# Block 0's inverse taken straight from the four products, pairs formed later, in a two-layer convolution and GeGLU kernel

## The chip, the cores and the metric

The kernel runs on one core of one Trainium2 chip. The metric is the device time of one execution in microseconds (us), lower is better. Each core has TensorE (PE: matrix multiplies from SBUF into PSUM), VectorE (DVE), ScalarE (ACT), GpSimd (POOL) and a queue of its own for transfers (SP). SBUF is the on-chip memory, PSUM the memory that matmuls accumulate into; the program holds three PSUM tiles of one kind (`ps`, `pr`) and one of another (`cps`).

## The reference

```python
x = A_q
x = x + A(layernorm(x)); x = x + B(layernorm(x))
x = x + A(layernorm(x)); x = x + B(layernorm(x))

A(q):  k_shift = sum over 4 taps of k (delayed by t) * shift_k[:, t]
       kv = k_shift * v
       y = causal convolution of kv with ssm_k, by FFT of length 2S, in bf16
       return q * (y + kv * ssm_D)
B(x):  return (gelu(x @ w_gate) * (x @ w_up)) @ w_down
```

S is 2048 and D is 576; the hidden width F is 4608. `y` doesn't depend on x, so the kernel computes it once for both layers. The operands are bf16.

## The kernel before

**Tiling.** The sequence is cut into four chunks of 512 rows, and each chunk into four tiles of 128 rows. The convolution works by chunk: a block's `kv` and a block's filter are taken to a frequency domain of four tables of 128 frequencies (`kt` 0 to 3, each with a real and an imaginary part, `part` or `s` 0 and 1), multiplied there, and taken back by `inverse` (L392), one row tile `mt` at a time. Forward and backward transforms are matmuls with constant tables `W`; some of them also stand in `W` with the sign turned.

**Units.** The MLP runs in 8 units (two layers, four chunks). In a unit, `gu` (L1583 for the first unit's first third, L1663 for the others) multiplies the normed, transposed rows `xnT` by gate and up weights, ScalarE takes the gelu, VectorE the product `hT`, and `dn` (L1697) multiplies by the down weights. Weights stream in over SP's queue (`load_wgu`, `load_wd`). From the first `gu` on, the convolution of the later chunks is filled into these units by a planner (`Pace`, `fill`) with cost figures of its own; the change gives the planner no new figure.

**The opening.** Ahead of the first `gu` the program runs `begin` (L817), in an order written out by hand; each engine works through its instructions in that order. It computes block 0 of the convolution (which needs only chunk 0 of k, v and the filter), turns the filter's block 1, and brings rows 0 and 2 of chunk 0 through gate, norm and transpose, since the first half of the first unit needs only those (rows 1 and 3 follow in `first_half`, L1520). Its steps:

- `even` and `odd` (L973, L980): the filter's spectrum for two tables, from even and from odd rows, into one PSUM tile; ScalarE copies out the even sum `eo` and then the total `h`, and `apart` (L985) gets the other table by `differ` (L230, VectorE): twice the even sum less the total. `kfwd` (L990) is the same for `kv`, copied out by ScalarE as `kc`.
- `kacc(kt)` (L1000) forms the complex product of `kc` and `h` for one table: two tiles `A[(part, kt)]`, each a product (L358 or L360) and a sum (L361) on VectorE.
- `straight` (L1014) accumulates rows 0 and 2 of the inverse from the four `A` tables, as they come, in PSUM tiles `Y[0]` and `Y[2]`.
- `pair0(kt, sg)` (L1007) forms on GpSimd, for both parts, the sum (`sg` 0) or the difference (`sg` 1) of `A[(part, kt)]` and `A[(part, kt + 2)]`. Rows 1 and 3 of the inverse are taken from the two differences by `terms` (L385): 8 matmuls a row. The four differences and four sums (`yb`) also serve later: block 1's inverse needs the pairs of the block before it, which `shifted` (L378) updates in place, one of them by an adding transfer.
- `gate` (L1471; two multiply-adds on VectorE, L1478 and L1481), `mean`, `sq` (ScalarE, L1204), `std` (ScalarE, L1498), `norm` (VectorE, L1422, and a small copy, L1424), `turn` (nine transposes on TensorE, L1443) and `copy` (L1450) bring a row to `xnT`. `keep_y` (L406, ScalarE) copies a finished row of the inverse out of PSUM. `busy` (L871) and `idle` (L1431) are matmuls and transposes whose results are not used.
- `turn_h(1)` and `copy_h` transpose the filter's block 1 into `hT1`. `put` writes spectra to DRAM over GpSimd's queue.

**After it.** `first_half` runs six `half_gu` units of 36 matmuls. Each takes one of the three PSUM tiles, as do the two transposed rows between the third, fourth and fifth of them; of the first four units VectorE's product (L1589) is the last to read the tile.

Of the kernel before, what the change touches and what calls it, by code (L numbers as in the profile page):

```python
# [85 lines left out]
class Conv:  # L86
# [283 lines left out]
    def both(self, kt, part, first, second):  # L370

        b = {}
        for sg, op in ((0, ALU.add), (1, ALU.subtract)):
            b[sg] = self.ybp.tile([P, self.D], BF16, tag="yb", name="yb")
            self.nc.vector.tensor_tensor(out=self.halves(b[sg][:]), in0=first, in1=second, op=op)
        return b

    def shifted(self, now, prev, part, transfer=False):  # L378
        if transfer and part == 1:
# [437 lines left out]
    def begin(self, head, tables):  # L817
# [4 lines left out]
        with ExitStack() as es:  # L822
# [8 lines left out]
            ones = tmp.tile([1, P], BF16, name="ones")  # L831
            warm = tmp.tile([P, 1], F32, name="warm")
            self.Wx = tmp.tile([P, 2, P], BF16, name="Wx")
            hn = [tmp.tile([P, nd + 1, BS], BF16, name=f"hn{b}") for b in range(2)]
            hT0 = tmp.tile([P, RT, D], BF16, name="hT0")
            kT = head.scratch([P, nt, RT, P + 2], "kT")
# [99 lines left out]
            def turn_h(b):  # L936

                hv = hn[b][:].rearrange("p b (q i) -> p b i q", i=RT)
                pt = [new_t() for g in range(2)]
# [10 lines left out]
            copy_h(hT0, turn_h(0), (0, 1))  # L950
# [29 lines left out]
            def odd(kt, s):  # L980
                ps, eo = E[kt, s]
                self.fwd_sum(ps, hT0, kt, s, 1)
                nc.scalar.copy(out=self.halves(h0[kt][:, s, :]), in_=ps[:, :, 0:HW])

            def apart(kt):  # L985
                for s in range(2):
                    ps, eo = E[kt, s]
                    self.differ(h0[kt + 2][:, s, :], eo, ps)

            def kfwd(kt, s, ps):  # L990
                if s == 0:
                    kc[kt] = self.kcp.tile([P, 2, D], BF16, tag="kc", name="kc")
                self.fwd_full(v, kt, s, kc[kt], ps=ps)

            def put(kt, *what):
                for w in what:
                    self.spill((self.Kd if w is kc else self.Hd)[0][kt], w[kt])
                self.flush(0.0)
# [5 lines left out]
                    A[(part, kt)] = t  # L1004
            self.yb, self.yb_of = {}, 0

            def pair0(kt, sg):  # L1007
                for part in range(2):
                    b = self.ybp.tile([P, D], BF16, tag="yb", name="yb")
                    nc.gpsimd.tensor_tensor(out=b[:], in0=A[(part, kt)][:], in1=A[(part, kt + 2)][:],  # L1010
                                            op=ALU.subtract if sg else ALU.add)
                    self.yb[(part, kt, sg)] = b

            def straight(mt, kts, first=False, last=False):  # L1014

                self.inverse(0, mt, [(self.inv_w(mt, s, mt == 2 and kt % 2 == 1), A[(s, kt)]) for kt in kts for s in range(2)],
                             Y[mt], first, last)

            even(0, 0)
            even(0, 1)  # L1020
            kfwd(0, 0, small())
            odd(0, 0)
            odd(0, 1)
            kfwd(0, 1, new())
            head.row_sum(0)
            head.row_sum(2)
            apart(0)
            head.row_sum(1)
            head.act_sq(0)
            kacc(0)  # L1030
# [11 lines left out]
            odd(1, 0)  # L1042
            odd(1, 1)
            kfwd(1, 1, new())
            pair0(0, 1)
            apart(1)
            kacc(1)
            put(1, h0, kc)
# [2 lines left out]
            head.act_sq(2)  # L1051
            kfwd(3, 1, new())
            self.load_v(1, nc.gpsimd)
            self.hT1 = head.scratch([P, RT, D], "hT1")
            copy_h(self.hT1, turn_h(1), (1, 0))
            Y = {0: new()}
            head.reserve(0)
            Y[2] = new()
            straight(0, (0, 2), True)
            straight(2, (0, 2), True)  # L1060
            straight(0, (1,))
            kacc(3)
# [30 lines left out]
            nc.scalar.activation(out=warm[:], in_=head.zero, func=ACT.Gelu_apprx_tanh)  # L1093
            pair0(0, 0)
            pair0(1, 0)
            head.gate(1, None, 0)
            self.startup = False


@with_exitstack  # L1100
def ssm_geglu_kernel(ctx, tc, A_q, A_k, A_v, A_shift_k, A_ssm_k, A_ssm_D, B_x, B_w_gate, B_w_up,
# [308 lines left out]
    with tc.manual_schedule():  # L1410
# [377 lines left out]
```

## Time and profile before

| | before |
|---|---|
| time, median of 3 runs | 921.23 us (920.99 to 921.79) |
| the profiled execution's own time | 921.34 us |
| its span, first to last instruction | 919.5 us |
| TensorE, VectorE, ScalarE, GpSimd busy | 906.3, 584.0, 331.0, 165.8 us |
| first `gu` matmul | at 45.56 us of the span |
| chain that ended last | TensorE 95%, VectorE 4% |
| mean granted TensorE clock | 0.994 |

Rows of the profile name an engine, a line of the kernel, an operation and its tiles: `out<-in`, then partitions x elements and type, then how many instructions the row holds. A row of the timeline begins with its start and its length in us; square brackets hold the idle time of the engine before it, with the instruction that ended it. The chain of waits is followed back from the last instruction, at each step to what released it. Time on engines that the chain does not pass costs nothing by itself. "Granted clock" is the share of full speed that TensorE was allowed.

### The profile page before, as it was taken

To read this page: it belongs to the slowest core of one execution; us is meant where nothing else is said; L and a number is where in the kernel's file an instruction comes from. 1 tells how busy PE (TensorE), PEld (TensorE's weight loads), DVE (VectorE), ACT (ScalarE), POOL (GpSimd) and SP (SyncE) were. 2 spreads that over 40 slices of the span, in tenths; PEclk is the share of its full clock that TensorE was granted. 3 is DMA by queue.
4 is the path that set the end of the run, shared out by engine and by line. 5 is a ranking of instruction groups with operands and counts; after the bars stand their busy time and mean duration, and the time that the engine had idled before them with its cause. 6 is when DMAs were issued, how large, how long until landed. Compare 5 with 4: busy or idle time off the path is not lost.

```text
span 919.5 us, 19224 instructions
## 1 busy us (share of the span) xinstructions
PE 906.3 (99%) x8167; PEld 527.4 (57%) x8167; DVE 584.0 (64%) x973; ACT 331.0 (36%) x619; POOL 165.8 (18%) x341
## 2 busy tenths in 40 slices
PE   9699999999999999999999999999999999999998
PEld 6487456465564564655645646646546556556555
DVE  7988897679889886597898864453333335332332
ACT  7465724633215145363123133551221224421211
POOL 3711423311114022240103102220000003100000
PEclk9899999999999999999999999999999999999999
DMA  9759997929627707993933810890720721977620
GB/s 257 264 192 219 321 234 134 251 91 218 182 79 153 215 1 141 243 159 69 263 96 99 182 43 27 157 179 2 155 78 1 155 79 24 165 174 169 143 64 26
DMA packets 128954, 131.14 MB, mean 143 GB/s; under 512 B 43618, under 2 KB 120675, under 8 KB 128868
## 3 DMA queue, kind: packets, MB, share of 16 engines
q1 hardware_dynamic: 119232, 93.47, 48.3%
q0 software_dynamic: 9632, 36.43, 12.2%
q8 instruction: 64, 1.05, 0.5%
q14 instruction: 22, 0.18, 0.1%
q10 hardware_dynamic: 4, 0.01, 0.0%
HBM read 108.35 MB, written 11.80 MB: 131 GB/s over the span
## 4 chain that ended last, share of the span: by engine, by line
PE 95%; DVE 4%; ACT 0%; issue 0%; DVEq 0%
PE gu L1663 59%; PE dn L1697 31%; PE gu L1583 3%; PE cps L281 1%; DVE yb L361 1%; DVE x_c L1481 1%; PE ps L401 1%; PE cps L401 0%; PE ps L281 0%; DVE h L232 0%; DVE prod L360 0%; DVE prod L358 0%; PE cps L873 0%; DVE v L965 0%; DVE wx L933 0%; DVE wx L932 0%
## 5 line engine op out<-in xcount | busy, mean ns | idle before, releaser
L1663 PE MATMUL gu<-xnT,wgu 64*128 64x512 bf16 x4968 | 540.7, 376 | 0.0
L1663 PEld LDWEIGHTS <-wgu 64*128 64x128 bf16 x4968 | 239.6, 94 | 294.4 <-issue 6.2
L1672 ACT ACTIVATE ga<-gu 128x512 f32<-128x512 f32 x258 | 153.9, 596 | 451.0 <-PE gu L1663 442.7
L1673 DVE TENSOR_TENSOR hT<-ga,gu 128x512 bf16<-128x512 f32 x258 | 176.8, 685 | 200.8 <-ACT ga L1672 199.2
L1697 PE MATMUL dn<-wd,hT 128*128 128x288 bf16 x2304 | 292.3, 286 | 0.0
L1697 PEld LDWEIGHTS <-hT 128*128 128x128 bf16 x2304 | 223.5, 98 | 65.6 <-issue 9.5
L1733 DVE TENSOR_TENSOR x_c<-x_c,dn 128x576 f32<-128x576 f32 x64 | 48.1, 752 | 57.2 <-PE dn L1697 56.9
L1196 POOL TENSOR_SCALAR nm<-s 128x1 f32<-128x1 f32 x60 | 21.2, 355 | 272.3 <-DVE x_c L1728 210.8
L1204 ACT ACTIVATE junk<-x_c,nm 128x576 bf16<-128x576 f32 x48 | 36.9, 768 | 35.6 <-POOL nm L1196 25.8
L1212 POOL TENSOR_TENSOR rstd<-ve,neghalf_t 128x1 f32<-128x1 f32 x62 | 40.0, 646 | 5.2
L541 POOL DMA_DIRECT2D hr<-Hd x32 | 17.4, 545 | 119.3 <-DVE prod L360 118.7
L1211 POOL TENSOR_SCALAR ve<-ss 128x1 f32<-128x1 f32 x62 | 22.9, 369 | 53.6 <-ACT junk L1204 53.5
L1268 ACT ACTIVATE xn<-x_c,nb,rstd 128x576 bf16<-128x576 f32 (+1 forms) x48 | 28.6, 644 | 5.8 <-POOL nb L1216 5.7
L284 ACT COPY eo<-cps 128x576 f32<-128x576 f32 x31 | 19.8, 640 | 28.0 <-PE cps L281 24.4
L1719 DVE TENSOR_TENSOR ob<-x_c,dn 128x576 bf16<-128x576 f32 x15 | 11.3, 753 | 29.0 <-PE dn L1697 26.2
L1562 ACT ACTIVATE ga<-gu 128x512 bf16<-128x512 f32 x26 | 15.5, 597 | 31.9 <-PE gu L1663 24.9
L1583 PE MATMUL gu<-xnT,wgu 64*128 64x256 bf16 x432 | 26.0, 278 | 0.6 <-ACT xnT L1450 0.6
L1583 PEld LDWEIGHTS <-wgu 64*128 64x128 bf16 x432 | 22.5, 97 | 3.5 <-issue 1.1
L416 POOL DMA_DIRECT2D out_dram<-ob x12 | 6.7, 562 | 91.8 <-DVE ob L1719 71.8
L361 DVE TENSOR_TENSOR prod<-prod 128x576 bf16<-128x576 bf16 x48 | 22.0, 458 | 1.6
L244 DVE SCALAR_TENSOR_TENSOR eo<-eo 128x576 f32<-128x576 f32 x22 | 16.3, 752 | 5.8 <-ACT eo L284 5.8
L1246 DVE SCALAR_TENSOR_TENSOR x_c<-g_t,rstd,x_c 128x576 f32<-128x576 f32 x16 | 13.0, 813 | 8.6 <-POOL rstd L1212 8.6
(163 smaller groups left out, 601.3 us busy)
## 6 DMA issues: line engine op xcount, KB each, us to landing
wgu<-in_B_w_gate_dram SPq DMA_DIRECT2D x45, 576.0 KB, 5.9
wd<-in_B_w_down_dram SPq DMA_DIRECT2D x30, 864.0 KB, 7.5
wgu<-in_B_w_up_dram SPq DMA_DIRECT2D x45, 512.0 KB, 7.7
hr<-Hd POOLq DMA_DIRECT2D x32, 288.0 KB, 5.5
kr<-Kd POOLq DMA_DIRECT2D x24, 288.0 KB, 5.7
Kd<-kc POOLq DMA_DIRECT2D x12, 288.0 KB, 6.5
k<-in_A_k_dram POOLq DMA_DIRECT2D x3, 1008.0 KB, 11.9
wgu<-in_B_w_up_dram SPq DMA_DIRECT2D x45, 64.0 KB, 7.3
```

Source lines behind the costliest of these rows:

```text
L361: nc.vector.tensor_tensor(out=dst, in0=pr[:, 0, :], in1=pr[:, 1, :], op=ALU.subtract if part == 0 else ALU.add)
L1196: nc.gpsimd.tensor_scalar(out=v["nm"][:], in0=v["s"][:], scalar1=-1.0 / D, scalar2=None, op0=ALU.mult)
L1204: nc.scalar.activation(out=junk[:], in_=get_x(), func=ACT.Square, bias=v["nm"][:, 0:1], accum_out=v["ss"][:])
L1211: nc.gpsimd.tensor_scalar(out=ve[:], in0=v["ss"][:], scalar1=1.0 / D, scalar2=EPS, op0=ALU.mult, op1=ALU.add)
L1212: nc.gpsimd.tensor_tensor(out=v["rstd"][:], in0=ve[:], in1=neghalf_t[:, 0:1], op=ALU.pow)
L1268: nc.scalar.activation(out=xn[:, lo:hi], in_=x_c[c][:, j, 0:hi - lo], func=ACT.Identity, scale=v["rstd"][:, 0:1], bias=v["nb"][:, 0:1])
L1583: nc.tensor.matmul(pair[:, s, e * 256:(e + 1) * 256], lhsT=w[r0:r0 + HK, k, gi * P:(gi + 1) * P], rhs=xnT[r0:r0 + HK, blk_of[k], tok], sta ...
L1663: nc.tensor.matmul(pair[:, s, :], lhsT=w[r0:r0 + HK, k, gi * P:(gi + 1) * P], rhs=xnT[r0:r0 + HK, b, :], start=(k == 0), stop=(k == NKC - 1))
L1672: nc.scalar.activation(out=ga[:], in_=pair[:, 0, :], func=ACT.Gelu_apprx_tanh)
L1673: nc.vector.tensor_tensor(out=hT[:, fi, :], in0=ga[:], in1=pair[:, 1, :], op=ALU.mult)
L1697: nc.tensor.matmul(part[h][:, h, 0:HW], lhsT=hT[:, fi, at * P:(at + 1) * P], rhs=wd[2 * wb + fi // WT][:, fi % WT, h * HW:(h + 1) * HW], s ...
L1733: nc.vector.tensor_tensor(out=xh, in0=xh, in1=acc[:, :, 0:HW], op=ALU.add)
```

## The change

Rows 1 and 3 of block 0's inverse are no longer taken from differences but straight from the four `A` tables like rows 0 and 2, as signed sums of 16 matmuls a row. Two tables with turned sign that `W` doesn't hold are made by ScalarE (`Wn`). `pair0` is gone. The four differences are formed by VectorE (`apart0`): one between the norms of rows 0 and 2, three in `first_half`. The four sums are formed by transfers on GpSimd's queue that add `A[(part, kt)]` into `A[(part, kt + 2)]` (`together0`), in `first_half` behind `load_x(1)`. The order of the opening changes too: block 0's `odd` ahead of its first `kfwd`; `apart(0)` ahead of two row sums; `turn_h(1)` takes one PSUM tile of the other kind; row 1's inverse comes ahead of row 0's `sq`, with two `keep_y`; row 3's is cut in three pieces set between norms and turns; ScalarE's table load for gelu comes ahead of the `xnT` copies, three of which are VectorE's now; the six `busy` matmuls and four of the ten `idle` transposes are gone.

```diff
+    def apart0(self, A, part, kt):
+        b = self.ybp.tile([P, self.D], BF16, tag="yb", name="yb")
+        self.nc.vector.tensor_tensor(out=b[:], in0=A[(part, kt)][:], in1=A[(part, kt + 2)][:], op=ALU.subtract)
+        self.yb[(part, kt, 1)] = b
+
+    def together0(self, A):
+        for kt in range(2):
+            for part in range(2):
+                self.nc.gpsimd.dma_start(out=A[(part, kt + 2)][:], in_=A[(part, kt)][:], accum_op=ALU.add)
+                self.yb[(part, kt, 0)] = A[(part, kt + 2)]
...
-            def straight(mt, kts, first=False, last=False):
-                self.inverse(0, mt, [(self.inv_w(mt, s, mt == 2 and kt % 2 == 1), A[(s, kt)]) for kt in kts for s in range(2)],
-                             Y[mt], first, last)
+            def straight(mt, kts, first=False, last=False, parts=(0, 1)):
+                terms = []
+                for kt in kts:
+                    for part in parts:
+                        if mt % 2 == 0:
+                            s, minus = part, mt == 2 and kt % 2 == 1
+                        elif kt % 2 == 0:
+                            s, minus = part, kt == 2
+                        else:
+                            s, minus = 1 - part, ((mt == 1) == (part == 1)) != (kt == 3)
+                        w = Wn[:, mt // 2, :] if minus and (mt, s) in ((1, 1), (3, 0)) else self.inv_w(mt, s, minus)
+                        terms.append((w, A[(part, kt)]))
+                self.inverse(0, mt, terms, Y[mt], first, last)
             even(0, 0)
             even(0, 1)
-            kfwd(0, 0, small())
             odd(0, 0)
             odd(0, 1)
+            kfwd(0, 0, small())
             kfwd(0, 1, new())
             head.row_sum(0)
+            apart(0)
             head.row_sum(2)
-            apart(0)
             head.row_sum(1)
...
-            pair0(0, 1)
             apart(1)
...
+            for e, at in enumerate((15, 18)):
+                nc.scalar.activation(out=Wn[:, e, :], in_=self.W[:, at, :], func=ACT.Copy, scale=-1.0)
             self.hT1 = head.scratch([P, RT, D], "hT1")
-            copy_h(self.hT1, turn_h(1), (1, 0))
+            copy_h(self.hT1, turn_h(1, (small_t(), new_t())), (1, 0))
             Y = {0: new()}
             head.reserve(0)
             Y[2] = new()
-            straight(0, (0, 2), True)
+            straight(0, (0, 2, 1), True)
             straight(2, (0, 2), True)
-            straight(0, (1,))
             kacc(3)
             straight(0, (3,), last=True)
             straight(2, (1, 3), last=True)
-            pair0(1, 1)
             head.act_sq(1)
             head.act_sq(3)
             head.gate(0, Y[0])
             head.mean(0)
             put(3, kc)
+            self.keep_y(0, 0, Y[0])
+            Y[1] = small()
+            straight(1, (0, 2, 1, 3), True, True)
+            self.keep_y(0, 1, Y[1])
+            head.idle(6)
             head.sq(0)
             head.std(0)
-            Y[1] = small()
-            busy(Y[1], 6)
-            self.inverse(0, 1, self.terms(1, self.yb), Y[1])
-            head.idle(10)
+            Y[3] = small()
+            straight(3, (0, 2), True)
             head.gate(2, Y[2])
             head.mean(2)
-            self.keep_y(0, 1, Y[1])
             head.sq(2)
             head.std(2)
-            Y[3] = small()
-            self.inverse(0, 3, self.terms(3, self.yb), Y[3])
             head.norm(0)
             head.turn(0)
-            nc.vector.tensor_copy(out=self.halves(self.y[0][:, 0, :]), in_=Y[0][:, :, 0:HW])
+            self.apart0(A, 0, 0)
+            straight(3, (1,))
+            head.norm(2)
+            nc.scalar.activation(out=warm[:], in_=head.zero, func=ACT.Gelu_apprx_tanh)
+            head.copy(0, nc.vector.tensor_copy)
+            head.turn(2)
+            straight(3, (3,), last=True)
+            head.copy(2, nc.scalar.copy, nc.vector.tensor_copy)
             self.keep_y(0, 3, Y[3])
-            head.norm(2)
-            head.copy(0, nc.scalar.copy, nc.vector.tensor_copy)
-            head.turn(2, small_t())
-            head.copy(2, nc.scalar.copy, nc.vector.tensor_copy)
             self.keep_y(0, 2, Y[2])
-            nc.scalar.activation(out=warm[:], in_=head.zero, func=ACT.Gelu_apprx_tanh)
-            pair0(0, 0)
-            pair0(1, 0)
             head.gate(1, None, 0)
...
             mean0(3)
+            conv.apart0(conv.A0, 1, 0)
             for n in range(FP // 2):
...
                     norm0(1)
+                    conv.apart0(conv.A0, 0, 1)
                 elif n == 1:
                     root0(3)
                     norm0(3)
+                    conv.apart0(conv.A0, 1, 1)
                     load_x(1)
+                    conv.together0(conv.A0)
```

More of the change, by code (lines that the diff above doesn't have):

```diff
@@ L833, in begin @@
             self.Wx = tmp.tile([P, 2, P], BF16, name="Wx")
+            Wn = tmp.tile([P, 2, P], BF16, name="Wn")
             hn = [tmp.tile([P, nd + 1, BS], BF16, name=f"hn{b}") for b in range(2)]
@@ L934, in begin, with turn_h @@
             tt(out=v[:, :, rest], in0=wx[0][:], in1=v[:, :, rest], op=ALU.mult)
-            def turn_h(b):
+            def turn_h(b, pt):
                 hv = hn[b][:].rearrange("p b (q i) -> p b i q", i=RT)
-                pt = [new_t() for g in range(2)]
                 for dbs in (range(nd), (nd,)):
@@ L949, in copy_h @@
                     nc.scalar.copy(out=hT[:, 2 * g:2 * g + 2, :], in_=pt[g][:, :, 0:D])
-            copy_h(hT0, turn_h(0), (0, 1))
+            copy_h(hT0, turn_h(0, (new_t(), new_t())), (0, 1))
             out = []
@@ L1005, in begin @@
             self.yb, self.yb_of = {}, 0
[L1007 to L1012, printed above, removed]
-            def straight(mt, kts, first=False, last=False):
-                self.inverse(0, mt, [(self.inv_w(mt, s, mt == 2 and kt % 2 == 1), A[(s, kt)]) for kt in kts for s in range(2)],
-                             Y[mt], first, last)
+            def straight(mt, kts, first=False, last=False, parts=(0, 1)):
[11 more added lines that the diff above has]
+                self.inverse(0, mt, terms, Y[mt], first, last)
             even(0, 0)
             even(0, 1)
-            kfwd(0, 0, small())
             odd(0, 0)
             odd(0, 1)
+            kfwd(0, 0, small())
             kfwd(0, 1, new())
             head.row_sum(0)
+            apart(0)
             head.row_sum(2)
-            apart(0)
             head.row_sum(1)
@@ L1070, in begin @@
             put(3, kc)
+            self.keep_y(0, 0, Y[0])
[3 more added lines that the diff above has]
+            head.idle(6)
             head.sq(0)
             head.std(0)
-            Y[1] = small()
-            busy(Y[1], 6)
-            self.inverse(0, 1, self.terms(1, self.yb), Y[1])
-            head.idle(10)
+            Y[3] = small()
+            straight(3, (0, 2), True)
             head.gate(2, Y[2])
             head.mean(2)
-            self.keep_y(0, 1, Y[1])
             head.sq(2)
             head.std(2)
-            Y[3] = small()
-            self.inverse(0, 3, self.terms(3, self.yb), Y[3])
             head.norm(0)
             head.turn(0)
-            nc.vector.tensor_copy(out=self.halves(self.y[0][:, 0, :]), in_=Y[0][:, :, 0:HW])
+            self.apart0(A, 0, 0)
[6 more added lines that the diff above has]
+            head.copy(2, nc.scalar.copy, nc.vector.tensor_copy)
             self.keep_y(0, 3, Y[3])
-            head.norm(2)
-            head.copy(0, nc.scalar.copy, nc.vector.tensor_copy)
-            head.turn(2, small_t())
-            head.copy(2, nc.scalar.copy, nc.vector.tensor_copy)
             self.keep_y(0, 2, Y[2])
-            nc.scalar.activation(out=warm[:], in_=head.zero, func=ACT.Gelu_apprx_tanh)
-            pair0(0, 0)
-            pair0(1, 0)
             head.gate(1, None, 0)
+            self.A0 = A
             self.startup = False
```

## The prediction

> **What bounds the kernel now.** I read the page first (TensorE is busy for 906.3 of 919.5 us, so only the opening can give much), then the chain of waits in order of time, cut at 60 us: whatever stands there ahead of the first `gu` matmul delays every later matmul by as much. Columns: start, length, what.
>
> ```profile
> 15.26 1.42 DVE h L232 x2
> 16.68 0.66 DVE s L1460
> 17.35 0.67 DVE prod L358
> ...
> 24.04 3.40 DVE yb L361
> ...
> 30.46 1.95 DVE yb L361
> ...
> 32.46 0.65 PE ps L401 x2
> ...
> 33.21 0.82 DVE x_c L1478
> ...
> 35.98 5.87 DVE x_c L1481 x2
> ...
> 45.56 7.43 PE gu L1583 x108
> ```
>
> From 15.26 to 45.56 the chain runs almost wholly through VectorE. Three of its pieces are far too long. The view of single lines says what one such instruction takes (minimum/median/maximum in ns), and the timeline says what GpSimd did meanwhile:
>
> ```profile
> L361 DVE TENSOR_TENSOR yb<-prod x8: 457/458/3402, 18.0 to 30.5; 128x576 bf16<-128x576 bf16 x8
> ```
> ```profile
> L1481 DVE SCALAR_TENSOR_TENSOR x_c<-x_c,rstd,x_b x4: 817/820/5847, 34.1 to 48.1; 128x576 f32<-128x576 f32 x4
> ```
> ```profile
> 24.60 2.52 POOL L1010 TENSOR_TENSOR yb<-yb 128x576 bf16<-128x576 bf16 x2
> ...
> 30.80 1.28 POOL L1010 TENSOR_TENSOR yb<-yb 128x576 bf16<-128x576 bf16 x1
> ...
> 32.48 1.27 POOL L1010 TENSOR_TENSOR yb<-yb 128x576 bf16<-128x576 bf16 x1 [0.40 <-DVE yb L361]
> ...
> 36.26 4.95 POOL L1010 TENSOR_TENSOR yb<-yb 128x576 bf16<-128x576 bf16 x4
> ```
>
> An addition of 0.46 us took 3.40 and 1.95, and a multiply-add of 0.82 took 5.85. Each time `pair0` ran on GpSimd, and the excess (2.94, 1.49, 5.03) is close to the length of that run (2.52, 1.28, 4.95). Once the GpSimd run ends, the VectorE instruction ends 0.3 to 0.6 us later. So **9.46 us of the chain are VectorE standing still behind GpSimd's tensor instructions.** Beside the one addition that stalled nothing (32.48) ran the `x_c` L1478 of 33.21, which reads one operand from PSUM.
>
> **The change part by part.** I walk the chain to two marks: the first `gu` matmul (45.56 before), and the sixth `gu` unit.
>
> *Order at the start.* `even` and `odd` of block 0 now come ahead of `kfwd`, and `apart(0)` ahead of two of the three row sums. The `odd` matmuls need only the ScalarE copies of the `even` sums:
>
> ```profile
> 11.85 1.18 ACT L978 COPY eo<-ps 128x576 f32<-128x576 f32 x2 [0.46 <-PE ps L227]
> ...
> 12.14 0.68 DVE L965 TENSOR_TENSOR v<-ps,v 128x512 bf16<-128x512 f32 x1
> ...
> 16.01 0.64 ACT L220 CAST kc<-ps 128x576 bf16<-128x576 f32 x1 [0.24 <-PE ps L218]
> ```
>
> The two copies end near 12.4 and 13.0, so the four `odd` matmuls of each end near 13.1 and 13.7, and their ScalarE copies near 13.7 and 14.3. VectorE does one row sum of 0.66 (12.82 to 13.5), both differences (1.42, from 13.7 to 15.1), two row sums (to 16.4). The second `kc` copy then ends near 16.35 (16.65 before: TensorE no longer waits for `v`). First product at 16.42 instead of 17.35: **-0.93 us**. It is kept if no `kc` is late afterwards: I get 22.2 for block 1's second (needed 22.4) and 24.5 for block 3's (needed 24.7). These are the thinnest margins of this part; if they fail, some 0.3 of the 0.93 comes back.
>
> *Differences off GpSimd.* The last product sum then ends at 32.41 - 0.93 - 2.94 - 1.49 = 27.05.
>
> *TensorE at the first gate.* The 0.65 us for two matmuls in the chain is a half-speed figure. Windows (length; TensorE, its weight loads, VectorE, ScalarE, GpSimd busy; granted clock, DMA share, GB/s), and two of the same matmuls before the clock fell:
>
> ```profile
> 30.00:32.00 2.00, 0.22 (x2) 0.03 (x1) 1.97 (x2) 0.00 (x0) 1.97 (x3) 0.83 1.04 335
> 32.00:34.00 2.00, 1.54 (x7) 0.99 (x7) 1.19 (x2) 0.00 (x0) 1.51 (x4) 0.50 0.98 354
> ...
> 40.00:42.00 2.00, 0.09 (x1) 0.00 (x0) 1.97 (x4) 0.00 (x0) 1.20 (x1) 1.00 0.15 57
> ...
> 46.00:48.00 2.00, 2.00 (x22) 1.62 (x20) 1.86 (x5) 1.97 (x4) 0.00 (x0) 0.50 0.00 0
> ```
> ```profile
> 28.66 0.40 PE L401 MATMUL ps<-yb,W 128*128 128x288 bf16 x2 [0.76 <-DVE yb L361]
> ```
>
> The clock fell to 0.50 after the near idle time around 30, which is now filled. Two matmuls at full clock took 0.40: **-0.25 us**. `gate(0)` starts at 27.6 (33.21 before).
>
> *Gates.* Unstalled, the two gates with their means take 3.78 us (33.21 to 36.99 with L1481 at 0.82): **-5.03 us**, ending at 31.4.
>
> *The new wait.* ScalarE now has `keep_y(0,0)` and `keep_y(0,1)` ahead of `sq(0)`, and `keep_y(0,1)` waits for 16 matmuls where the pairs needed 8. Rows:
>
> ```profile
> 35.27 0.78 ACT L1204 ACTIVATE junk<-x_c,nm 128x576 bf16<-128x576 f32 x1 [6.57 <-DVE nm L1487]
> ...
> 36.23 0.29 ACT L1498 ACTIVATE std<-ss,eps_t 128x1 f32<-128x1 f32 x1
> ...
> 38.25 0.65 ACT L407 ACTIVATE y<-cps 128x576 bf16<-128x576 f32 x1 [1.72 <-PE cps L401]
> ...
> 38.95 1.14 PE L401 MATMUL cps<-yb,W 128*128 128x288 bf16 x8
> ```
>
> Eight matmuls cost 0.97 in a row and end 0.17 later (1.14). Behind row 0's last ones (27.5) stand 8 for row 2 and 16 for row 1, so row 1 is done at 30.6; its copy ends at 31.3, `sq` and `std` (1.25 from start to end) at 32.55. Queued behind on ScalarE are `sq(2)`, `std(2)` (33.8), and on VectorE `norm(0)` waits: 1.2 us later than its gates allow. **+1.2 us**.
>
> *The tail.*
> ```profile
> 41.94 0.15 DVE L1421 RECIPROCAL rstd<-std 128x1 f32<-128x1 f32 x1
> ...
> 42.74 0.18 DVE L1424 COPY xn<-xn 128x64 bf16<-128x64 bf16 x1
> ```
> `norm(0)` takes 0.98 from reciprocal to copy: to 33.55. `apart0` is an L361 shape: +0.46, to 34.0, past `std(2)`. `norm(2)` to 35.05. Then VectorE copies three pieces of `xnT` where two engines shared four:
>
> ```profile
> 44.53 0.42 DVE L1450 COPY xnT<-xps 128x512 bf16<-128x512 bf16 x1
> 44.82 0.69 ACT L1450 COPY xnT<-xps 128x640 bf16<-128x640 bf16 x1 [0.33 <-PE xps L1443]
> ...
> 46.08 1.28 ACT L1093 ACT_TABLE_LOAD   x1
> ```
>
> 0.42 twice, and 0.49 for the 640 (by size from 0.42): to 36.4. ScalarE's table load (33.8 to 35.3) lies beside `norm(2)`, and its one copy ends at 36.05. From the first reciprocal to `gu` this is 3.9 us against 3.6 before: **+0.2 us**. `gu` starts at **36.5**: 9.1 us earlier.
>
> *No row of its own:* the two `Wn` copies of 128x128. Between a ScalarE instruction of one element (0.29) and the 128x512 one (0.60) two cost 0.6 to 1.2; I take 0.6, nearest to the smaller. They delay block 1's copies, row 2's first matmuls and so `gate(0)` by 0 to 0.6; the 24.5 above leaves room for the first 0.5, so I charge 0.
>
> *First units.* Three more `apart0` (0.46 each) stand in VectorE's queue, with the products that free the PSUM tiles of the first units queued behind them. The sixth unit needs the tile that the fourth product (57.98) frees. The means of the last two gates ended at 49.15:
>
> ```profile
> 49.00 0.15 DVE L1487 TENSOR_SCALAR nm<-s 128x1 f32<-128x1 f32 x1
> ...
> 53.66 0.69 DVE L1589 TENSOR_TENSOR hT<-ga,gu 128x512 bf16<-128x512 f32 x1 [0.57 <-ACT ga L1588]
> ...
> 57.98 0.68 DVE L1589 TENSOR_TENSOR hT<-ga,gu 128x512 bf16<-128x512 f32 x1
> ```
> ```profile
> 56.70 6.11 PE L1583 MATMUL gu<-xnT,wgu 64*128 64x256 bf16 x108
> ```
>
> The last row is three units, five to seven, of 2.04 each. Before, the sixth started at 58.74, 0.1 us after that product. After, VectorE has no gap: from 36.4, gates 3.8 (to 49.15 from 45.4, right behind the `xnT` copies), three differences 1.4, three products 2.1, two norms 1.5, and from the third product's end (54.35) to the fourth's (58.66) 4.3 as before: 49.55. TensorE at full clock would be there at 48.4: five units of 2.04, and 1.67 for the two visits between them (from 52.99, the end of the chain's 108, to 56.70, less one unit). At the half clock of 46 to 48, worth 7.43 - 6.11 = 1.3, it is there at 49.7. So the three gaps of 0.57 that VectorE had ahead of these products go to the differences, and **what a warmer TensorE gains is lost to VectorE**: sixth unit at 49.6 against 58.74, **-9.15 us**.
>
> *Sums by transfer.* Four transfers on GpSimd's queue stand ahead of two `kr` loads, with some 3 us of issue and waiting. What GpSimd does next after those loads, and the first reader of a sum:
>
> ```profile
> 85.59 0.54 POOL L411 DMA_DIRECT2D Hd<-H  x1 [32.06 <-DVE H L253]
> ```
> ```profile
> L382 DVE TENSOR_TENSOR yb<-yb x6: 447/450/452, 109.9 to 136.0; 128x576 bf16<-128x576 bf16 x6
> ```
>
> GpSimd idles 32 us behind the loads, and sums issued near 45 are read at 101 at the earliest: no cost. Nothing behind the sixth unit changes its order. Sum: 921.34 (the profiled execution; 0.11 above the median of 921.23) - 9.15 = **912.2**.
>
> On TensorE's clock the Trainium skill (TensorE: Matmul & The Clock Gate, "What's actually happening" and Part 4) speaks against the change: a window of about 3.4 us without activity halves the clock, and transposes do not count as activity. The trace agrees on the idle window: from 40 to 42 TensorE was busy 0.09 us, and from 46 to 48 the clock is 0.50. By that rule the removed warming matmuls matter, and the time would be the cold rival's below.
>
> On the stall it says (GPSIMD Engine Reference, Specifications) that GpSimd shares its SBUF interface with VectorE instructions that have two SBUF inputs. The three stalled ones have two, L1478 has one. By that rule the stalls end with `pair0`; without it the first rival stands.
>
> **Rivals.**
> 1. *The stalls stay.* If DMA traffic stalls VectorE (share 1.04 from 30 to 32), 9.46 comes back: 912.2 + 9.5 = **921.7**. Against it: L1481 still stood from 40 to 41.8, with the share down to 0.15. 3%.
> 2. *VectorE does not bind the first units.* Then the warm clock's part is kept (48.4 for 49.6): **911.0**. It would need VectorE to save 1.2 in an unbroken queue. 12%.
> 3. *TensorE goes cold in the tail*, between 31 and 36.5, where I count about 1.5 us of plain matmuls. The tail's last eight double (+0.5), and the units reach the sixth 0.1 to 0.5 later: **913.0**. 15%.
> 4. *The margins fail* (late `kc`, `Wn` at 1.2, row 1's copy later): up to 1.5 more, **913.7**. 12%.
> 5. *Slower: the third weight tile.*
> ```profile
> 20.27 3.33 SPq L1160 DMA_DIRECT2D wgu<-in_B_w_up_dram  x1
> ```
> ```profile
> wgu<-in_B_w_up_dram SPq DMA_DIRECT2D x1, 64.0 KB, 22.2
> ```
> Its last part landed at 42.5. The fifth unit needs it at 46.3 after (56.7 before), and as VectorE holds the sixth it may come 1.2 later: decisive from 47.5. The three `wd` loads (864 KB each), which wait for the opening's scratch memory, now start near 36, in the midst of the backlog. All 2.6 MB ahead of it at 354 GB/s are 7.3 us: 49.8, **914.5**. Slower by over 0.2% (923.1) needs it at 58.4. 3%.
>
> **How the numbers follow.** My forecast (the sum, within 0.7) has 55%. Range 910.3 to 914.6: it takes in rivals 2, 3 and 4 and leaves out 1, the slower end of 5, and slips between. A measurement can tell about 0.2%, 1.8 us, from no change: faster 0.95 (all cases but 1 and 5's far end), same 0.03, slower 0.02.
>
> **What would show it.** L361 at 0.46 and L1481 at 0.82 throughout; last product sum at 27; `gu` at 36.5; ScalarE idle before `keep_y(0,1)`; TensorE waiting about 1 us for `hT` L1589 (its line shifts) ahead of the sixth unit, or a clock of 0.50 at `gu`. Wrong if long L361 or L1481 remain, if `gu` starts after 38, or if it waits for `wgu`.

## The result and the profile after

The kernel after took 912.56 us (median; 911.78 to 913.03) beside 921.25 (920.99 to 921.79) for the kernel before: ratio 0.9904, 95% interval 0.9887 to 0.9921, or 8.7 us less. Measured a second time it took 912.53 beside 921.68 (0.9899, 0.9885 to 0.9914). The profiled execution took 912.86 us, its span is 911.0, and its granted clock 1.000 (0.994 before).

The view of single lines of the kernel after (minimum/median/maximum in ns) has no long addition and no long multiply-add left; L1497 is the old L1481:

```profile
L361 DVE TENSOR_TENSOR yb<-prod x8: 457/458/486, 18.6 to 28.1; 128x576 bf16<-128x576 bf16 x8
```
```profile
L1497 DVE SCALAR_TENSOR_TENSOR x_c<-x_c,rstd,x_b x4: 817/818/819, 30.1 to 40.5; 128x576 f32<-128x576 f32 x4
```

The chain of waits of the kernel after, in order of time, cut at 60 us (start, length, what):

```profile
7.41 2.04 PE pt L957 x20
...
13.14 0.65 ACT eo L991
...
13.84 1.19 PE ps L227 x8
15.03 0.98 PE cps L218 x8
...
25.97 4.05 PE ps L414 x32
30.02 1.97 PE cps L414 x16
...
32.02 0.04 ACT y L420
32.06 0.50 issue
32.56 0.86 ACT junk L1220 x2
...
33.51 0.30 ACT std L1514
...
34.04 0.59 DVE xn L1438
...
36.66 0.70 ACT xnT L1466
...
41.42 0.06 DVE yb L381
...
41.79 0.68 DVE hT L1609
...
45.20 0.60 DVE hT L1609
...
49.51 0.61 DVE hT L1609
...
50.16 4.11 PE gu L1603 x72
```

Before, VectorE carried this chain from 15.3 us to the first `gu`. Now TensorE does, from 13.84 to 32.0, in rows of 0.98 us for eight matmuls without a gap: the transforms and then the 48 matmuls of three inverse rows. Behind it stand row 1's copy (`keep_y`, L420), row 0's `sq` and `std`, and the norm. From 37.8 to 50.1 VectorE carries it, up to the product (49.51) that the sixth unit (50.16; 58.74 before) waits for.

The head of the chain is not the change's doing. The 20 transposes `pt` (unchanged code) and what follows make the first `eo` copy start at 13.14, where it started at 11.85 before. So I give marks from here on as distances from that copy. The sixth unit stood 46.89 us behind it before and stands 37.02 behind it after: **9.87 us gained, 1.29 lost in the front.**

### The profile page after: what moved, and what is told of

It is laid out like the page before. It is cut to its first block, busy times and chain, and to the rows that moved or that the text cites. A ratio compares the mean times of both kernels' runs of the same rounds, so it can differ in the third digit from the quotient of the medians.

```text
span 911.0 us, 19242 instructions
## 1 busy us (share of the span) xinstructions
PE 904.1 (99%) x8173; PEld 527.1 (58%) x8173; DVE 576.0 (63%) x977; ACT 331.2 (36%) x621; POOL 159.3 (17%) x337
## 3 DMA queue, kind: packets, MB, share of 16 engines
q1 hardware_dynamic: 119232, 93.47, 49.6%
q0 software_dynamic: 10208, 37.02, 12.9%
## 4 chain that ended last, share of the span: by engine, by line
PE 98%; DVE 2%; ACT 0%; issue 0%; DVEq 0%; ACTq 0%
PE gu L1683 59%; PE dn L1717 31%; PE gu L1603 2%; PE ps L414 1%; PE cps L281 1%; PE cps L414 1%; PE cps L218 0%; PE ps L281 0%; PE ps L218 0%; PE ps L227 0%; PE cps L887 0%; PE pt L957 0%; DVE hT L1609 0%; PE cps L817 0%; DVE xn L1438 0%; DVE kvt L193 0%
```

## The experiments

"Front" is the start of the first `eo` copy in the profiled execution, "sixth" the distance from there to the sixth `gu` unit.

| kernel | median us (range) | ratio, 95% interval | front | sixth |
|---|---|---|---|---|
| before, first profile | 921.25 (920.99 to 921.79) | | 11.85 | 46.89 |
| y3_before_again | 922.04 (921.38 to 923.40) | 1.0003 (0.9994 to 1.0013) | 13.13 | 46.83 |
| after | 912.56 (911.78 to 913.03) | 0.9904 (0.9887 to 0.9921) | 13.14 | 37.02 |
| a0_again | 912.53 (911.54 to 912.75) | 0.9899 (0.9885 to 0.9914) | 13.06 | 37.02 |
| x1_no_sums | 916.34 (914.30 to 917.57) | 0.9938 (0.9922 to 0.9954) | 12.70 | 40.41 |
| x2_pool_copies | 918.97 (915.57 to 919.30) | 0.9963 (0.9950 to 0.9976) | 12.43 | 43.82 |
| x3_first_order | 912.66 (912.42 to 913.12) | 0.9904 (0.9889 to 0.9918) | 13.23 | 37.20 |
| x4_std_first | 911.75 (911.24 to 912.02) | 0.9893 (0.9877 to 0.9910) | 12.60 | 36.23 |
| y1_std_first_again | 911.66 (911.29 to 912.01) | 0.9889 (0.9871 to 0.9906) | 13.09 | 36.23 |
| x5_no_later_differences | 912.10 (911.16 to 912.31) | 0.9895 (0.9880 to 0.9910) | 12.97 | 36.41 |
| x6_differences_on_pool | 914.87 (914.63 to 915.46) | 0.9926 (0.9911 to 0.9940) | 12.19 | 39.71 |
| x7_pairs_on_dve | 911.26 (911.23 to 911.49) | 0.9886 (0.9870 to 0.9903) | 11.99 | 36.52 |
| y2_pairs_on_dve_again | 911.26 (911.15 to 912.16) | 0.9888 (0.9872 to 0.9903) | 13.32 | 36.17 |
| y4_std_first_late_pairs | 910.71 (910.31 to 911.80) | 0.9881 (0.9866 to 0.9897) | 13.42 | 35.64 |

Where the trace joins the units to one row, the sixth's start is the row's start plus 2.04 for each unit ahead of it. Each ratio is against executions of the kernel before beside it. The names with "again" repeat a kernel without an edit; a0_again is the kernel after.

In all fourteen profiled executions the execution's time less the start of the sixth unit (front plus sixth) is 862.6 to 862.9 us. So what sets these kernels apart, the front included, happens ahead of that unit, and the distance shows a kernel's own part of it. The medians also hold executions whose front no profile shows.

> The changed kernel once more, as the base for the three beside it. If the 1.5 us that its TensorE waited for the last part of the filter's block 0 (20 transposes took 2.25 us instead of 1.43) is chance, this profile has the first eo copy near 11.9 instead of 13.14, the first gu near 36.6 and the sixth unit near 49.3, and a time near 911.9; if it belongs to the changed kernel, the profile repeats 13.1, 37.9, 50.2 and 912.9.

### Is it GpSimd? The kernel before with one thing taken away

**x1_no_sums.** The four sums are not formed; block 1 reads `A[(part, kt + 2)]` in their place, so that its part of the output is not the reference's.

```diff
-            pair0(0, 0)
-            pair0(1, 0)
+            for kt in range(2):
+                for part in range(2):
+                    self.yb[(part, kt, 0)] = A[(part, kt + 2)]
```

> The kernel before without the four sums that GpSimd formed beside the gates (block 1's inverse gets plain tables in their place, so the output differs). Theory, GpSimd's tensor instructions stop VectorE's instructions with two SBUF inputs: L1481 takes 0.82 everywhere, gate(2) ends 5.0 earlier, std(2) is then held by row 1's copy (38.9), so the second norm starts 3.3 earlier and the time falls by 3 to 5, to 916 to 918. Rival, DMA traffic stops VectorE: the 5.85 us of L1481 stays, and the time stays within 1 of 921.3.

Measured: 5.4 us less, for sums that occupied GpSimd for 4.95. The multiply-adds of the two gates in VectorE's timeline:

```profile
31.98 2.65 DVE L1482 SCALAR_TENSOR_TENSOR x_c<-x_c,rstd,x_b 128x576 f32<-128x576 f32 x1
...
35.65 0.82 DVE L1482 SCALAR_TENSOR_TENSOR x_c<-x_c,rstd,x_b 128x576 f32<-128x576 f32 x1
```

The second, which had taken 5.85, took 0.82. The forecast of 0.82 everywhere didn't hold: the two pairs of differences went on stopping VectorE, elsewhere than in the first profile. An addition at 25.55 took 1.51, a product at 26.98 took 1.83 for 0.75, and the first gate's multiply-add 2.65. In the profile the sixth unit stands 6.48 nearer to the front; 1.27 of that is the first row of `gu`, which took 6.16 us for 7.43.

**x2_pool_copies.** GpSimd copies one table where it added two. Block 1 again reads other data than the reference's.

```diff
-            pair0(0, 0)
-            pair0(1, 0)
+            for kt in range(2):
+                for part in range(2):
+                    b = self.ybp.tile([P, D], BF16, tag="yb", name="yb")
+                    nc.gpsimd.tensor_copy(out=b[:], in_=A[(part, kt)][:])
+                    self.yb[(part, kt, 0)] = b
```

> The kernel before with the four sums replaced by four copies of the same size on GpSimd (one input; block 1's inverse gets plain tables, so the output differs). If any GpSimd tensor instruction stops VectorE's two-input ones, L1481 takes 0.82 plus about the length of the four copies, and the time lies between x1_no_sums and the kernel before, by that length. If only GpSimd instructions with two inputs do, L1481 takes 0.82 and the time is that of x1_no_sums. If VectorE is stopped for a fixed time, 921.3.

The timelines of GpSimd and of VectorE in this kernel:

```profile
36.80 2.48 POOL L1097 COPY yb<-yb 128x576 bf16<-128x576 bf16 x4
```
```profile
36.87 2.73 DVE L1425 TENSOR_SCALAR xn<-x_c,nm,rstd 128x576 bf16<-128x576 f32 x1
...
40.59 0.58 DVE L1425 TENSOR_SCALAR xn<-x_c,nm,rstd 128x576 bf16<-128x576 f32 x1
```

Copies have one operand, and they stop VectorE all the same. What they stopped is not the second gate's multiply-add, which took 0.82, but a norm, which reads one tensor from SBUF: 2.73 us for 0.58. The median lies 2.63 above x1_no_sums, for copies that took 2.48, though the ranges overlap. In the profiles the sixth unit stands 3.41 further back than in x1_no_sums, and 1.62 of that is the first row of `gu` (7.78 us for 6.16), which began at a granted clock of 0.50.

**x6_differences_on_pool.** The kernel after, with its four differences back on GpSimd.

```diff
-        self.nc.vector.tensor_tensor(out=b[:], in0=A[(part, kt)][:], in1=A[(part, kt + 2)][:], op=ALU.subtract)
+        self.nc.gpsimd.tensor_tensor(out=b[:], in0=A[(part, kt)][:], in1=A[(part, kt + 2)][:], op=ALU.subtract)
```

> The changed kernel with its four differences on GpSimd instead of VectorE. Theory: each takes 1.28 there and stops a VectorE instruction with two SBUF inputs beside it; the first lies beside norm(0) and norm(2), which have one SBUF input, and costs nothing unless they are stopped too; the other three lie beside gates, products with a PSUM input and the taps, and the adding transfers wait for them. VectorE is relieved of 1.8 but stopped up to 3.8: sixth unit between 0.5 earlier and 2.0 later, time -0.5 to +2.0 against the changed kernel. If norms are stopped as well, gu is 0.8 later than in the changed kernel.

It took 2.3 us more than the kernel after, and my upper figure fell short: it counted neither stopped norms nor TensorE's clock. GpSimd, VectorE and the windows (columns as in the prediction) in this kernel:

```profile
32.04 2.51 POOL L381 TENSOR_TENSOR yb<-yb 128x576 bf16<-128x576 bf16 x2
...
45.14 1.27 POOL L381 TENSOR_TENSOR yb<-yb 128x576 bf16<-128x576 bf16 x1
```
```profile
33.09 1.79 DVE L1438 TENSOR_SCALAR xn<-x_c,nm,rstd 128x576 bf16<-128x576 f32 x1
...
45.21 1.52 DVE L1438 TENSOR_SCALAR xn<-x_c,nm,rstd 128x576 bf16<-128x576 f32 x1
```
```profile
32.00:34.00 2.00, 0.91 (x8) 0.49 (x5) 1.08 (x2) 1.82 (x6) 1.97 (x3) 1.00 1.00 351
34.00:36.00 2.00, 1.06 (x12) 0.88 (x13) 1.90 (x6) 1.49 (x3) 0.56 (x1) 0.87 1.02 393
36.00:38.00 2.00, 2.00 (x15) 1.61 (x14) 0.73 (x2) 0.41 (x1) 0.00 (x0) 0.50 1.04 409
```

With the norm stopped TensorE was busy for only 0.91 and 1.06 us of two windows, and its clock read 0.87 and then 0.50. `gu` ran on 26.26 us behind the front for 24.72 after: 1.54 later, where stopped norms alone had been put at 0.8.

### Which part of the change brings the gain?

**x7_pairs_on_dve** and **y2_pairs_on_dve_again.** The kernel before with only the engines of the pairs changed: `pair0` runs on VectorE at its old places for the differences, and the sums are the adding transfers. Inverse, tail and order of the start stay as before.

```diff
-                    nc.gpsimd.tensor_tensor(out=b[:], in0=A[(part, kt)][:], in1=A[(part, kt + 2)][:],
+                    nc.vector.tensor_tensor(out=b[:], in0=A[(part, kt)][:], in1=A[(part, kt + 2)][:],
...
-            pair0(0, 0)
-            pair0(1, 0)
...
+            self.A0 = A
...
                     load_x(1)
+                    for kt in range(2):
+                        for part in range(2):
+                            A = conv.A0
+                            nc.gpsimd.dma_start(out=A[(part, kt + 2)][:], in_=A[(part, kt)][:], accum_op=ALU.add)
+                            conv.yb[(part, kt, 0)] = A[(part, kt + 2)]
```

> The kernel before with the four differences on VectorE at their places instead of GpSimd, and the four sums by adding transfers as in the changed kernel: rows 1 and 3 still come from differences with 8 matmuls a row, and no other order changes. Theory: 9.46 us of stalls go, four differences of 0.46 come on VectorE's chain (+1.8), the clock stays up (-0.3): -7.9, about 913.4, that is, most of the change is the removal of GpSimd's instructions, and the straight inverse with its new order is worth the last 1. Rival: the straight inverse is what frees the chain (row 1 no longer waits for pairs), and this one stays above 915.

> The kernel before with its four differences on VectorE and the sums by adding transfers, run once more. Chance: eo anywhere from 11.8 to 13.3, the sixth gu unit 36.6 us after it, the median 910.9 to 912.1. Of the kernel: eo at 12.0 again and 911.2 to 911.5. If it stays under the kernel after (912.5) by about 1 us in another call, the rearranged inverse of the change costs time by itself.

Both times the median was 911.26, under the forecast of the first and 1.3 below the kernel after. So taking the tensor instructions off GpSimd is by itself enough for all of the gain. It is also more than was forecast: in the first profile the sixth unit stands 10.37 us nearer to the front than before, for 7.9. Two terms were off. One is TensorE's clock, which the forecast left out for `gu`: its first three units took 6.07 us, and 7.43 before, where the clock read 0.50.

```profile
36.69 6.07 PE L1587 MATMUL gu<-xnT,wgu 64*128 64x256 bf16 x108 [0.56 <-ACT xnT L1449]
```
```profile
38.00:40.00 2.00, 2.00 (x42) 2.00 (x39) 1.86 (x5) 1.94 (x5) 0.44 (x1) 1.00 1.06 380
```

The other is the differences, put at 1.8:

```profile
L1010 DVE TENSOR_TENSOR yb<-yb x4: 451/452/453, 21.9 to 29.0; 128x576 bf16<-128x576 bf16 x4
```

Two of them stand on the chain, with 0.74 together as they overlap. The other two lie where VectorE waits for TensorE's last matmuls anyway (0.81 us before, 0.58 after). In y2_pairs_on_dve_again, whose front is as late as that of the kernel after, `gate(0)` starts 1.01 us later behind it (30.35 - 13.32 against 29.16 - 13.14). But by the first `gu` the kernel after has nothing left of that: 24.70 and 24.34 behind the front in the two profiles here, 24.72 there (37.86, behind two early matmuls). The next two experiments show where it went.

**x4_std_first** and **y1_std_first_again.** The kernel after with the new wait taken off row 0's path.

```diff
-            self.keep_y(0, 1, Y[1])
             head.idle(6)
             head.sq(0)
             head.std(0)
+            self.keep_y(0, 1, Y[1])
```

> The changed kernel with the copy of row 1 of the inverse moved behind sq and std of row 0 on ScalarE. Theory: that copy's wait for 16 matmuls is the +1.2 us of the sum; std(0) ends 1.2 to 1.4 earlier, norm(0) starts when its gates end (0.9 earlier), std(2) 0.7 earlier, the first gu and the sixth unit 0.7 to 0.9 earlier, time 0.8 below the changed kernel. Rival: row 3's inverse, which waits for that copy's PSUM tile, or VectorE's copies take its place, and the time moves by less than 0.2.

> The kernel after with row 0's sq and std ahead of row 1's copy, run once more. Two theories of why the first eo copy began at 13.14 in the kernel after and at 11.85 before, though the code ahead of it is the same. Chance: the matmuls run at half rate (17 transposes per us for 25) until a moment that differs from one execution to the next by up to some 3 us (7.6 us before, 10 after, 9.0 in this kernel's first profile); then eo lies anywhere from 11.8 to 13.3 here, each us by which that moment is later costs 0.5, and the sixth gu unit begins 36.2 us after eo as in its first profile (36.23). Of the kernel: eo at 12.6 again, within 0.1. The time is 911.2 to 912.0 by both.

0.8 to 0.9 us less, and the sixth unit 0.79 nearer to the front, in both profiles alike. ScalarE's timeline after and here:

```profile
32.02 0.65 ACT L420 ACTIVATE y<-cps 128x576 bf16<-128x576 f32 x1 [1.36 <-PE cps L414]
32.56 0.77 ACT L1220 ACTIVATE junk<-x_c,nm 128x576 bf16<-128x576 f32 x1
```
```profile
30.68 0.78 ACT L1220 ACTIVATE junk<-x_c,nm 128x576 bf16<-128x576 f32 x1 [0.56 <-DVE nm L1503]
...
31.64 0.30 ACT L1514 ACTIVATE std<-ss,eps_t 128x1 f32<-128x1 f32 x1
31.84 0.63 ACT L420 ACTIVATE y<-cps 128x576 bf16<-128x576 f32 x1
```

After, ScalarE idles 1.36 us for row 1's sixteen matmuls with `sq` queued behind its copy; here `sq` follows the gate, and the copy finds the matmuls done.

**x5_no_later_differences.** The kernel after without the three differences in `first_half`; block 1 reads the tables in their place, so that its part of the output is not the reference's.

```diff
-            conv.apart0(conv.A0, 1, 0)
+            for p, q in ((1, 0), (0, 1), (1, 1)):
+                conv.yb[(p, q, 1)] = conv.A0[(p, q)]
...
-                    conv.apart0(conv.A0, 0, 1)
...
-                    conv.apart0(conv.A0, 1, 1)
```

> The changed kernel without the three differences in the first units: block 1's inverse gets the plain tables in their place, so the output differs. Theory: VectorE binds up to the sixth unit; without 1.2 to 1.4 us of its work the fourth product ends that much earlier, TensorE's wait of 0.49 us ahead of the sixth unit goes, and the time falls by 0.5, no more, since TensorE is then the bound. Rival: VectorE's products wait for the gelu anyway (ScalarE), the wait stays, and the time is the same within 0.1.

**y4_std_first_late_pairs.** x4_std_first, with the three differences and the adding transfers moved behind the fourth product.

```diff
-            conv.apart0(conv.A0, 1, 0)
...
                 if n == 3:
                     t.on_dve(C_HT, t.on_act(C_GELU, t.pe + 0.15) + 0.15)
+                    for part, kt in ((1, 0), (0, 1), (1, 1)):
+                        conv.apart0(conv.A0, part, kt)
+                    conv.together0(conv.A0)
...
-                    conv.apart0(conv.A0, 0, 1)
...
-                    conv.apart0(conv.A0, 1, 1)
...
-                    conv.together0(conv.A0)
```

> The kernel after with row 0's sq and std ahead of row 1's copy, and with the three later differences and the four adding transfers set behind the fourth product of the first half, so that no product that frees a PSUM tile is queued behind them. Theory (VectorE binds the sixth unit, the differences are the 0.5 us): sixth unit 35.7 us after eo (36.23 with the std alone moved), no wait for hT ahead of it, time 0.4 to 0.6 below y1_std_first_again, 910.9 to 911.5. Rival (TensorE binds by then, the differences have room): the same time as y1_std_first_again within 0.15. Rival on the other side: the sums now land later than a reader needs them, or the differences hold up the products of the fifth and sixth unit: 0.5 or more above it.

TensorE's timeline around the sixth unit: the kernel after, then without the differences, then with them late.

```profile
47.53 2.14 PE L1603 MATMUL gu<-xnT,wgu 64*128 64x256 bf16 x36
50.16 4.09 PE L1603 MATMUL gu<-xnT,wgu 64*128 64x256 bf16 x71 [0.49 <-DVE hT L1609]
```
```profile
47.34 6.11 PE L1602 MATMUL gu<-xnT,wgu 64*128 64x256 bf16 x108
```
```profile
47.02 6.12 PE L1602 MATMUL gu<-xnT,wgu 64*128 64x256 bf16 x108
```

The idle 0.49 us before the sixth unit is gone in both: three units run as one row. The sixth unit comes 0.61 and, against x4_std_first, 0.59 nearer to the front. VectorE bound it, and by the differences. y4_std_first_late_pairs, at 910.71, is the fastest kernel here, 1.85 below the kernel after; its 0.95 below y1_std_first_again is more than the 0.4 to 0.6 I had named, with ranges that overlap.

**x3_first_order.** The kernel after with the start in its old order.

```diff
+            kfwd(0, 0, small())
             odd(0, 0)
             odd(0, 1)
-            kfwd(0, 0, small())
             kfwd(0, 1, new())
             head.row_sum(0)
-            apart(0)
             head.row_sum(2)
+            apart(0)
```

> The changed kernel with the order at the start as it was (kfwd ahead of odd, the differences behind two row sums). Theory of the prediction, VectorE sets the pace there: first product 0.8 to 0.9 later against its eo copies, and the whole kernel 0.8 slower than the changed one. Rival, TensorE sets the pace from there to the inverse (its chain now runs through TensorE from 13.84 to 32.0): only the wait of the first kfwd for v comes back, 0.2 to 0.5 slower. Second rival: no difference, below 0.1.

0.13 us more in the median, with ranges that overlap, and 0.18 in the sixth unit's distance: a little under the first rival's 0.2 to 0.5. Behind a front as late as these two (13.06 and 13.23) the new order is worth 0.2.

### Why was the front later?

> The kernel before, unchanged, against itself: ratio 1.000 within 0.002. Chance: eo anywhere from 11.8 to 13.3. Of the kernel: eo at 11.85 within 0.1. The sixth gu unit begins 46.9 us after eo by both.

The second profile of the kernel before had its front at 13.13 where the first had 11.85, and the two of x7_pairs_on_dve 11.99 and 13.32. One program does both, so a late front needs no change in the kernel. Whether the changed kernels have it more often the profiles don't settle: it lies at 11.85 to 13.32 in the six that keep the old inverse and at 12.19 to 13.42 in the other eight. TensorE's timeline and its windows (length; TensorE, its weight loads, VectorE, ScalarE, GpSimd busy; granted clock, DMA share, GB/s) in the two profiles of x7_pairs_on_dve, the earlier front first:

```profile
7.16 1.58 PE L944 MATMUL pt<-ident,hn 128*128 128x128 bf16 x20
```
```profile
6.00:8.00 2.00, 2.00 (x24) 2.00 (x23) 1.97 (x8) 1.72 (x4) 0.85 (x2) 1.00 0.95 375
```
```profile
7.83 2.25 PE L944 MATMUL pt<-ident,hn 128*128 128x128 bf16 x20
```
```profile
6.00:8.00 2.00, 2.00 (x19) 1.92 (x18) 1.77 (x7) 1.36 (x6) 0.75 (x2) 1.00 1.00 387
```

The later one starts its transposes 0.67 us later and takes 0.67 longer for them. The granted clock reads 1.00 in both, so the slower transposes show in their lengths alone. The Trainium skill (TensorE: Matmul & The Clock Gate, "What's actually happening") says that the gate opens after a busy window of about 3.4 us which runs freely and does not restart with the kernel, so that the moment differs from execution to execution. The slower lengths agree with it; that this is their cause was not tried, and the later start isn't explained. The execution with the late front took 912.16 us, the one with the early front 911.23. Its sixth unit came 0.98 later, not 1.33, since the first product follows `eo` by 5.26 us in the early one and by 4.90 in the late one.

The second profile of the kernel before also shows the stalls at other places, beside GpSimd runs of 2.52, 2.51 and 4.95 us. VectorE's timeline in y3_before_again:

```profile
25.99 2.99 DVE L361 TENSOR_TENSOR yb<-prod 128x576 bf16<-128x576 bf16 x1
...
32.81 2.66 DVE L1481 SCALAR_TENSOR_TENSOR x_c<-x_c,rstd,x_b 128x576 f32<-128x576 f32 x1
...
37.62 5.23 DVE L1422 TENSOR_SCALAR xn<-x_c,nm,rstd 128x576 bf16<-128x576 f32 x1
```

The excess is 2.53, 1.84 and 4.65: 9.02 in all where the first profile had 9.46. The sixth unit's distance is the same within 0.06.

## Why the prediction was right, point by point

- *The stalls (-9.46).* Right. All eight additions took 0.46 to 0.49 and all four multiply-adds 0.82, and x7_pairs_on_dve gets the whole gain from taking GpSimd's instructions away: 9.46 by the stalls and 1.36 by the clock at `gu`, less 0.74 for its own differences. Which instructions stand still differs between executions; the sum is 9.46 in one and 9.02 in the other. The first rival, DMA traffic as the cause, falls: in the windows of the kernel after (columns as above) the share stands near or above 1 with no VectorE instruction stopped.

```profile
30.00:32.00 2.00, 2.00 (x21) 1.63 (x19) 1.77 (x5) 0.65 (x1) 1.80 (x5) 1.00 1.06 345
32.00:34.00 2.00, 1.46 (x14) 0.88 (x11) 1.07 (x4) 1.89 (x5) 0.96 (x2) 1.00 1.04 372
34.00:36.00 2.00, 1.22 (x14) 0.87 (x15) 1.86 (x7) 1.89 (x4) 0.00 (x0) 1.00 0.97 363
36.00:38.00 2.00, 1.54 (x19) 1.08 (x21) 1.45 (x5) 1.80 (x5) 0.00 (x0) 1.00 1.04 410
```

- *Order at the start (-0.93).* Mis-sized. The first product came at 17.85, not 16.42: 1.29 of that is the front, which I had taken from one profile as fixed. And behind the front the step gains 0.2: 4.71 us from `eo` to the first product after, 4.90 in x3_first_order, 4.91 in y3_before_again. The 5.41 of the first profile of before (17.26 in VectorE's timeline) belongs to its early front, in which TensorE had to wait for VectorE's `v`; x7_pairs_on_dve, as early, has 5.26. The new order keeps 4.71 with an early front too (x6_differences_on_pool, front 12.19), so there it would be worth 0.55 to 0.7. The term was sized for an early front and met a late one.
- *First gate and gates.* 16.02 and 19.80 behind the front, forecast 15.75 and 19.55: 0.25 too early, the start's share. The length of the gates, 3.78, is exact, and no cold clock came.
- *The new wait (+1.2).* Right in kind and close in size. `std(0)` ended 20.66 behind the front, forecast 20.70, and VectorE waited 0.90 for it. As the gates ended 0.25 later than forecast, that much of the 1.2 was already gone; x4_std_first gets 0.8 back.
- *Tail (+0.2) and the two `Wn` copies (0).* `gu` ran on 24.72 behind the front, forecast 24.65. The copies ended at 26.2, and TensorE's rows from 24.83 to 32.0 have no gap, so no wait shows for them.
- *First units (VectorE binds).* Right in kind; the wait was 0.49 us for my 1. I added up row lengths for gates, differences, products and norms, but successive VectorE instructions overlap: in the chain the stretch from the first late difference to the third product's end (41.42 to 45.80) is 4.4 us, and my terms for it are 1.4 + 2.1 + 1.5 = 5.0. The gates ahead of it took 3.6 for 3.8. So the sixth unit stood 37.02 behind the front, not 37.75. And the bold sentence, that VectorE takes what a warmer TensorE gains, holds for about a third: from `gu` to the sixth unit it took 13.18 before, 12.30 after and 11.82 in x7_pairs_on_dve, so 0.48 of 1.36 was lost and 0.88 kept.
- *Sums by transfer (0).* Right: no engine is listed as waiting for one, and from the sixth unit to the end the kernel after takes 862.7 us where the kernel before took 862.6.
- *Rivals.* The cold tail didn't come: the clock is 1.00 in all the windows above, with TensorE busy for 61 to 77% of the last three. The half clock priced at 913.0 was not seen here; in x6_differences_on_pool, at 46 and 53%, the clock did fall. Nor does the kernel after wait for the third weight tile.

The forecast was 912.2 for 912.56, and that it came so close is in part luck: two errors stand against each other. The front was 1.29 us later than I had it, and behind it I had 0.73 too much: the first units 0.8 too long, `gu` 0.1 too early (the 0.25 at the start was taken up by the new wait). Together they make the 0.56 by which the sixth unit came later, 50.16 for 49.6.

## What to carry to other kernels

Read a VectorE row whose maximum is several times its median beside GpSimd's timeline: if a GpSimd tensor instruction over whole tiles ends just before it does, move that instruction to VectorE or to an adding transfer first, and see what is left before anything is rearranged. Look also at TensorE's clock behind the stall: it was worth 1.36 here. That small edit alone gave 911.26. The rearrangement around it cost 1.3 in the medians (0.5 to 0.85 in the sixth unit's distance), until its wait (0.8) and the place of its differences (0.6) were mended. Take two profiles of a kernel before sizing a step of under 1 us near the start, and give marks from a point behind the part that varies.

## What the runs showed of the hardware

- A GpSimd copy (0.62 us for 128x576 bf16) stops VectorE as an addition does (1.27), and it stops a norm with one tensor operand in SBUF (0.58 became 2.73, 1.79 and 5.23 us). The Trainium skill (GPSIMD Engine Reference, Specifications) names instructions with two SBUF inputs or in a 2-port mode; which of its two cases the norm is, if either, the runs don't show. The one VectorE instruction with an operand in PSUM that ran beside such a run, the gate's first multiply-add, took 0.81 as always. GpSimd's instructions on 128x1 elements stopped nothing visible: one of 0.56 at 33.99 in the kernel before lies beside a multiply-add of 0.82.
- The granted clock of the profile read 1.00 while 20 transposes took 1.58 us in one execution and 2.25 in another of the same program.
- TensorE at 61 to 77% busy for 6 us kept its full clock in the kernel after, with no matmuls for warming (six idle transposes were left). At 46 and 53% busy for 4 us, in x6_differences_on_pool, its clock read 1.00, then 0.87, and 0.50 in the next window.
